# Gate/up and down as two passes over 512 tokens, weights loaded anew, seven PSUM banks in a ring, residual in bf16

## The chip, the core and the metric

The kernel runs on one core of a Trainium2 chip. A core has a matrix engine (PE in the profile, with its weight loads as PEld), a vector engine (DVE), a scalar engine (ACT), a general engine (POOL) and a queue engine that starts transfers (SP). Each executes its own instructions in the order in which the program wrote them; they wait for each other through semaphores. Data lie in SBUF, matrix products are summed in PSUM (eight banks of 512 fp32 numbers in each of 128 partitions). The metric is the device time of one execution in microseconds (us); before the change its median over 3 runs is 1082.35 us (1081.86 to 1082.96).

## What is computed

2048 tokens of width 576 pass through four layers: attention, gated unit, attention, gated unit, each with a layer norm in front and a residual sum behind. Both attention layers share their weights, and so do both gated units.

```python
x = x + A(layernorm(x))   # qkv = x @ wqkv (576 x 1728); 32 heads of 18; every token attends to
                          # 8 tokens: itself and those 2, 4, ... 14 before it; softmax; @ wo
x = x + B(layernorm(x))   # g = x @ w_gate; u = x @ w_up (576 x 4608); (g * u) @ w_down (4608 x 576)
```

The gated unit has most of the arithmetic; there is no nonlinear function in it, only the product `g * u`.

## The kernel before, in words

**Steps.** The tokens are cut into 18 steps: the first four of 128 tokens, the others of 256. The first half of the tokens passes both layers (steps 0 to 5 are attention layer 0 with its gated unit, 6 to 9 layer 1), then the second half (10 to 13, 14 to 17). `attention(j, ...)` and `glu(j, ...)` write the two halves of step `j`. All weights stay in SBUF, except `w_down`, which is loaded anew in each step, 18 tiles of 256 rows, into six buffers.

**Gate and up.** The 4608 inner columns are 36 column tiles of 128, and the 576 inputs are four full slices of 128 rows and one tail of 64. A unit is 512 PSUM columns of gate (one bank) and 512 of up (one bank): two column tiles at 256 tokens, four at 128. `full` (L788 to L796) multiplies the four full slices. `tails` (L798 to L809) multiplies the tails of two units at once: gate's 64 rows lie in the upper half of the array and up's in the lower, so that the two run side by side, in another division of the array than `full`. Units go in pairs: first one's `full`, `tails` of both, second one's `full`. In `evac` (L811 to L818) ACT copies g from PSUM to SBUF (L815) and DVE multiplies it with u out of PSUM (L816), which gives `h` in bf16.

**Down.** `down` (L826 to L836) multiplies `h` with `w_down` into `acc` (512 columns for each 128 tokens) and `acct` (the remaining 64). It runs behind the next pair's gate/up, in the same pass: pair by pair, gate/up and the down of the pair before alternate on PE. Gate/up has four PSUM banks, down three, and one, `pa`, is left to the small products of attention.

**Attention.** In `head` the layer norm (L353) is followed by a transpose, on PE in the first steps and by a DMA (L379) later. `project` (L458) computes q, k and v, in the same unit banks as gate/up. DVE forms q times k for the eight offsets (L580 to L590) in `prod` and `s1`; from step 5 on the sums over a head go through DRAM (`s_dram`, L641 to L647), softmax follows (L650 to L670), the weights go through DRAM once more (`a_dram` to `ab`, L691 to L694), DVE multiplies them with v and sums (L714, L731), PE multiplies with `wo` (L746), DVE adds the residual (L752), and the second `head` makes `xnT_B`, the input of the step's gated unit. The buffers `prod` and `s1` serve q times k, the returned parts, the softmax sums and the products with v of one step after the other; `a_c`, the weights, is a part of `s1`.

**Order.** `Plan` (L21 to L136) lists all operations with estimated costs, dependencies, priorities and buffers, and puts them in an order: each time it takes the operation that can start earliest. `bb` (L781) chains gate/up and down on PE in the order written; attention's products are put between them where their inputs and banks are planned to be ready, with margins (`mg`, 1500 ns in later steps). On the chip this order is fixed on each engine. Waits of SP for a buffer stand in the same queue as the transfers of attention.

Of the kernel before, what the change touches and what calls it, by code (L numbers as in the profile page):

```python
# [139 lines left out]
def kernel(  # L140
# [33 lines left out]
    NXS, NWD, NH, NXB = 4, 6, 4, 3  # L174
# [20 lines left out]
    wg = sb("wg", [P, KF, F])  # L195
    wu = sb("wu", [P, KF, F])
    wgu_t = sb("wgu_t", [P, F])
    Esel = sb("Esel", [P, 32])
    Bsel = sb("Bsel", [P, 4, 4, 32])
    xf = [sb(f"xf{i}", [P, NST, D], FP32) for i in range(NXS)]  # L200
    xb = [sb(f"xb{i}", [P, NST, D]) for i in range(2)]
    ob = [sb(f"ob{i}", [P, NST, D]) for i in range(2)]
# [7 lines left out]
    xnT_A = sb("xnT_A", [P, KT, CH])  # L210
    xnT_B = [sb(f"xnT_B{i}", [P, KT, CH]) for i in range(NXB)]
# [9 lines left out]
    wd = [sb(f"wd{i}", [P, 2, D]) for i in range(NWD)]  # L221

    pg = [psum.tile([P, 2 * CH], FP32, name=f"pg{i}") for i in range(2)]
    pu = [psum.tile([P, 2 * CH], FP32, name=f"pu{i}") for i in range(2)]
    acc = [psum.tile([P, 512], FP32, name=f"acc{i}") for i in range(NST)]
    acct = psum.tile([P, 512], FP32, name="acct")
    pa = psum.tile([P, 512], FP32, name="pa")

# [8 lines left out]
    banks = {"pa": [pa[:]], "boot": [acc[0][:], acc[1][:], acct[:]]}  # L237
    pool = {"k": "boot"}
# [24 lines left out]
    def load_x(t0, nst):  # L263
        b, i0 = (t0 // 2) % 2, t0 % 2
        if t0 == 2:
            op("POOL", 80, lambda: nc.gpsimd.memset(xb[b][0:1, i0, 0:2], 0.0), r=["wq3_0"], w=[f"xb{b}_{i0}"])
        o = op("SP", 600, dma(xb[b][:, i0:i0 + nst, :], xv[:, t0:t0 + nst, :]), w=[f"xb{b}_{i}" for i in range(i0, i0 + nst)],
               nbytes=P * nst * D * 2, prio=1.5 if t0 > 1 else 0, land=3000 if t0 else 1500, after=marks.get("x") if t0 == 3 else None)
        if t0 in (2, 3):
            marks["x"] = o  # L270
# [13 lines left out]
    def setup_b():  # L284
# [38 lines left out]
        def swap():  # L323
# [5 lines left out]
            late["a_c"] = late["s1"][:, 0:2 * CH]  # L329
            late["ab"] = rot.tile([P, 4, 2 * CH], BF16, name="ab")  # L330
        op("POOL", 0, swap, r=[f"wq{t}_{k}" for t in range(4) for k in range(KT)],
           w=["prod0", "prod1", "s10", "s11", "s12", "s13", "Lt", "ab"])
# [10 lines left out]
    def setup_glu():  # L343
        fw = F // FS
        for s in range(FS):
            fs = slice(s * fw, (s + 1) * fw)
            for nm, dst, src in (("wg", wg, B_w_gate), ("wu", wu, B_w_up)):
                op("SP", 500, dma(dst[:, :, fs], src[0:KF * P, fs].rearrange("(k p) f -> p k f", p=P)),
                   w=[f"{nm}{s}"], nbytes=P * KF * fw * 2, prio=4 + s, after=marks["x"])
            op("SP", 550, dma(wgu_t[0:TL, fs], B_w_gate[KF * P:D, fs]), w=[f"wgt{s}"], nbytes=TL * fw * 2, prio=4 + s, after=marks["x"])  # L350
            op("SP", 550, dma(wgu_t[TL:2 * TL, fs], B_w_up[KF * P:D, fs]), w=[f"wut{s}"], nbytes=TL * fw * 2, prio=4 + s, after=marks["x"])

    def head(src, keys, nst, dst, key, prio, ab, on_pe, mg, first=None, then=None):  # L353
# [18 lines left out]
        for i in range(nst):  # L372
# [5 lines left out]
            if not on_pe:  # L378
                op("SP", 900, lambda i=i: nc.sync.dma_start_transpose(out=dst[:, :, i * P:(i + 1) * P], in_=xn[i][:]),  # L379
                   r=[f"xn{ab}{i}"], w=[key + str(i)], prio=0, nbytes=P * KT * P * 2, land=2700)  # L380
                continue
# [6 lines left out]
            pl.also(o, [key + str(i)])  # L388
            o = op("ACT", 700, lambda i=i, b=b: nc.scalar.copy(dst[:, :, i * P:(i + 1) * P], bf(b())), r=[b.key], w=[key + str(i)],
# [49 lines left out]
    def attention(j, la, t0, nst):  # L439
        fast = j == 0  # L440
        z = j % 2
        qT, kT, vT = qT_[z], kT_[z], vT_[z]
# [4 lines left out]
        xs_b, xs_f = xb[(t0 // 2) % 2], xf[(t0 // 2) % NXS]  # L447
        bk = [f"xb{(t0 // 2) % 2}_{i0 + i}" for i in range(nst)]
        fk = [f"xf{(t0 // 2) % NXS}_{i0 + i}" for i in range(nst)]
        xin, xin_k = (xs_b, bk) if la == 0 else (xs_f, fk)  # L450
        xk = [f"xA{i}" for i in range(nst)]
        head(lambda i: xin[:, i0 + i, :], xin_k, nst, xnT_A, "xA", prio, 0, on_pe, mg, marks.get({2: "weights", 3: "sum"}.get(j)), marks["evac"] if j == 1 else None)
        op("ACT", 250, lambda: nc.scalar.copy(kT[:, :, 0:HALO], halo_k[la][:]), r=[f"halok{la}"], w=[f"kH{z}"], prio=prio)

        def bank(p_, u):
            return (pg, pu)[p_][u["slot"]]
# [69 lines left out]
        op("ACT", 250, lambda: nc.scalar.copy(vT[:, :, 0:HALO], halo_v[la][:]), r=[f"halov{la}"], w=[f"vH{z}"], prio=prio)  # L526
# [29 lines left out]
        else:  # L556
# [3 lines left out]
            project("a", uq, uv + ut, tq, ev_a, ev_b, [f"{x}{z}" for x in ("q0", "k0", "q2", "k2", "v0", "v2", "q4", "k4", "v4")])  # L560
        for d_, dst, hl in (("k", kT, halo_k), ("v", vT, halo_v)):
            op("ACT", 250, lambda hl=hl, dst=dst: nc.scalar.copy(hl[la][:], dst[:, :, n:n + HALO]),
               r=[f"{d_}{t}{z}" for t in range(0, KT, 2)], w=[f"halo{d_}{la}"], prio=prio)
# [7 lines left out]

        b1 = Bank()
# [357 lines left out]
```

## Time and profile before

| | |
|---|---|
| median of 3 runs | 1082.35 us |
| the profiled execution, its own time | 1079.86 us |
| span of its instructions | 1078.1 us |
| PE / DVE / ACT busy | 1063.8 / 755.1 / 369.4 us |
| matmuls | 10797 |
| `w_down` loads of 288 KB | 324 |
| first gate matmul / last matmul start | 32.7 / 1073.35 us |

The profile shows one execution. Its time is 1.8 us above its span (what lies around the first and the last instruction) and 2.5 us below the median of the runs. A row of a group names the source line, the engine, the operation, output and inputs with their shapes and the count; behind the bar come busy time in us and the mean of one in ns, then the idle time of the engine just before them with what ended it. A matmul's duration contains its way through the array, and matmuls overlap: what one costs in a sequence is read from one start to the next. A row of the timeline has start and duration in us; a row of the window table has the window, its length, and for each engine busy time and instructions. In the first 33 us the weights begin to arrive and the first attention runs; gate/up starts behind it.

### The profile page before, as it was taken

The numbers are of one execution on the slowest core, as the hardware profiler recorded it, in microseconds if no ns is written. First come the engines' busy times: TensorE is split into PE (matmuls) and PEld (weight loads), VectorE is DVE, ScalarE is ACT, GpSimd is POOL, SyncE is SP. The second block draws the span as 40 slices with busy tenths as digits, with TensorE's granted clock in tenths as the row PEclk, the third lists the DMA queues.
The fourth block names the chain that finished last, engine by engine and source line by source line (L and its number), as shares of the span: only waits on it lengthen the run. The fifth ranks groups of instructions, "written<-read, shape, count | busy, mean of one in ns | idle before, by whom it ended". The sixth has DMA issues, their size and how long they took to land.

```text
span 1078.1 us, 25413 instructions
## 1 busy us (share of the span) xinstructions
PE 1063.8 (99%) x10797; PEld 787.7 (73%) x10797; DVE 755.1 (70%) x1345; ACT 369.4 (34%) x756; POOL 8.8 (1%) x39
## 2 busy tenths in 40 slices
PE   8999999999999999999999999999999999999998
PEld 6788877777777777777777777777777777777775
DVE  7677987786959776685967778595876869472222
ACT  6544254332421544131242332423243332212121
POOL 3000000000000000000000000000000000000000
PEclk9999999999999999999999999999999999999999
DMA  9973774645263644435363734536353543534331
GB/s 278 342 208 92 208 175 122 169 105 138 79 169 105 153 115 108 126 112 150 109 170 97 162 93 121 134 84 170 89 153 91 127 116 106 157 112 112 101 110 56
DMA packets 155089, 146.16 MB, mean 136 GB/s; under 512 B 43104, under 2 KB 152672, under 8 KB 154976
## 3 DMA queue, kind: packets, MB, share of 16 engines
q1 hardware_dynamic: 154976, 144.55, 49.6%
q8 instruction: 84, 1.38, 0.5%
q14 instruction: 29, 0.24, 0.1%
HBM read 125.11 MB, written 10.88 MB: 126 GB/s over the span
## 4 chain that ended last, share of the span: by engine, by line
PE 95%; DMA 2%; DVE 2%; SPq 1%; issue 1%; ACT 0%; DVEq 0%; ACTq 0%
PE pg L793 24%; PE pu L793 23%; PE acc L832 23%; PE pg L804 7%; PE pg L469 5%; PE pu L469 4%; PE pa L746 4%; PE acct L834 3%; DMA wraw<-in_A_wqkv_dram 1%; DMA a_dram<-s 1%; DMA ab<-a_dram 1%; DVE h L816 0%; SPq L257 0%; DVE prod L714 0%; PE pa L680 0%
## 5 line engine op out<-in xcount | busy, mean ns | idle before, releaser
L816 DVE TENSOR_TENSOR h<-pu,g_sb 128x512 bf16<-128x512 f32 x288 | 196.3, 686 | 200.8 <-ACT g_sb L815 149.6
L815 ACT CAST g_sb<-pg 128x512 bf16<-128x512 f32 x288 | 168.2, 585 | 476.6 <-PE pu L804 391.3
L832 PE MATMUL acc<-wd,h 128*128 128x512 bf16 x1152 | 306.3, 380 | 0.0
L793 PE MATMUL pg<-xnT_B,wg 128*128 128x256 bf16 (+1 forms) x2592 | 300.8, 261 | 0.8 <-ACT xnT_B L431 0.8
L793 PE MATMUL pu<-xnT_B,wu 128*128 128x256 bf16 (+1 forms) x2592 | 299.3, 261 | 0.0
L793 PEld LDWEIGHTS <-wg 128*128 128x128 bf16 x2592 | 212.5, 98 | 61.2 <-issue 26.2
L793 PEld LDWEIGHTS <-wu 128*128 128x128 bf16 x2592 | 230.9, 98 | 23.3
L834 PE MATMUL acct<-wd,h 128*128 128x64 bf16 x1152 | 222.0, 193 | 0.0
L832 PEld LDWEIGHTS <-h 128*128 128x128 bf16 x1152 | 112.7, 98 | 117.9
L714 DVE TENSOR_TENSOR prod<-vT,ab 128x1280 bf16<-128x1280 bf16 (+1 forms) x127 | 92.9, 741 | 66.5 <-DMA ab<-a_dram 66.4
L469 PEld LDWEIGHTS <-wqkv 128*128 128x128 bf16 (+1 forms) x1260 | 95.4, 97 | 30.3 <-issue 16.1
L834 PEld LDWEIGHTS <-h 128*128 128x128 bf16 x1152 | 112.9, 98 | 2.2
L580 DVE TENSOR_TENSOR prod<-qT,kT 128x2560 bf16<-128x2560 bf16 (+1 forms) x72 | 95.5, 1331 | 1.0 <-ACT kT L522 0.4
L731 DVE TENSOR_TENSOR oT<-oT,prod 128x1280 bf16<-128x1280 bf16 (+1 forms) x119 | 90.8, 763 | 3.0
L804 PE MATMUL pu<-xnT_B,wgu_t 64*128 64x256 bf16 (+1 forms) x648 | 88.1, 260 | 0.0
L804 PE MATMUL pg<-xnT_B,wgu_t 64*128 64x256 bf16 (+1 forms) x648 | 88.0, 260 | 0.0
L469 PE MATMUL pg<-xnT_A,wqkv 128*128 128x256 bf16 (+3 forms) x650 | 79.7, 260 | 1.5 <-issue 0.9
L469 PE MATMUL pu<-xnT_A,wqkv 128*128 128x256 bf16 (+3 forms) x610 | 76.5, 262 | 2.6 <-DVE h L816 2.1
L804 PEld LDWEIGHTS <-wgu_t 64*128 64x128 bf16 x1296 | 47.0, 94 | 32.5 <-issue 27.8
L746 PE MATMUL pa<-wo_p,oT 128*128 128x288 bf16 x310 | 48.2, 286 | 0.1
L375 ACT ACTIVATE xn<-xf,nmr,rstd 128x576 bf16<-128x576 f32 x47 | 40.7, 866 | 8.8 <-DVE nmr L367 8.8
L584 DVE TENSOR_TENSOR prod<-prod 128x1024 bf16<-128x1024 bf16 (+1 forms) x64 | 41.1, 643 | 0.8
(117 smaller groups left out, 563.1 us busy)
## 6 DMA issues: line engine op xcount, KB each, us to landing
wd<-in_B_w_down_dram SPq DMA_DIRECT2D x324, 288.0 KB, 3.3
s_dram<-s SPq DMA_DIRECT2D x13, 512.0 KB, 3.7
prod<-s_dram SPq DMA_DIRECT2D x52, 128.0 KB, 2.9
ab<-a_dram SPq DMA_DIRECT2D x52, 128.0 KB, 2.7
wg<-in_B_w_gate_dram SPq DMA_DIRECT2D x6, 768.0 KB, 9.8
wu<-in_B_w_up_dram SPq DMA_DIRECT2D x6, 768.0 KB, 10.4
out_dram<-ob SPq DMA_DIRECT2D x8, 288.0 KB, 2.6
wraw<-in_A_wqkv_dram SPq DMA_DIRECT2D x4, 432.0 KB, 5.0
```

The lines of the kernel that those rows point to most:

```text
L469: nc.tensor.matmul(bank(p_, u)[0:m, e * n:(e + 1) * n], lhsT=wqkv[r_, k, c0:c0 + m], rhs=xnT_A[r_, k, 0:n], start=start, stop=stop, skip_g ...
L580: nc.vector.tensor_tensor(late["prod"][p_ % 2][:, :, :, 0:n], q2, k2, op=ALU.mult)
L584: nc.vector.tensor_tensor(prod[:, :, 0:4:2, 0:n], prod[:, :, 0:4:2, 0:n], prod[:, :, 1:4:2, 0:n], op=ALU.add)
L714: nc.vector.tensor_tensor(js(dst), js(vT[:, :, o0:o0 + n]), abw, op=ALU.mult)
L731: op("DVE", 60 + 3 * n, lambda i_=i_: nc.vector.tensor_tensor(oT[:, :, 0:n], oT[:, :, 0:n], late["prod"][i_ % 2][:, 0, :, 0:n], op=ALU.add ...
L746: nc.tensor.matmul(b()[:, 0:HD], lhsT=oT[:, t, i * P:(i + 1) * P], rhs=wo_p[:, t, hh * HD:(hh + 1) * HD], start=(t == 0), stop=(t == KT - 1))
L793: nc.tensor.matmul(pt[:, e * n:(e + 1) * n], lhsT=w_[:, k, ft * P:(ft + 1) * P], rhs=xT[:, k, 0:n], start=(first and k == 0 and e == 0), s ...
L804: nc.tensor.matmul(ps[:, e * n:(e + 1) * n], lhsT=wgu_t[r_, ft * P:(ft + 1) * P], rhs=xT[r_, KF, 0:n], start=(first and e == 0), stop=not ...
L815: op("ACT", 590, lambda: nc.scalar.copy(g_sb[gs][:, 0:ul], pg[use["slot"]][:, 0:ul]), r=[f"wg_{j}_{u}"], w=[f"g{gs}"], prio=0)
L816: op("DVE", 690, lambda: nc.vector.tensor_tensor(hb[hs][:, 0:ul], pu[use["slot"]][:, 0:ul], g_sb[gs][:, 0:ul], op=ALU.mult), r=[f"wu_{j}_{ ...
L832: nc.tensor.matmul(acc[i][:], lhsT=lhs, rhs=wt[:, e % 2, 0:512], start=(ft == 0), stop=(ft == NFT - 1))
L834: nc.tensor.matmul(acct[:, i * TL:(i + 1) * TL], lhsT=lhs, rhs=wt[:, e % 2, 512:D], start=(ft == 0 and i == 0), stop=(ft == NFT - 1), skip ...
```

## The change

Steps 0 to 5 stay in form. Everything after them (12 steps of 256 tokens) becomes six blocks of 512 tokens, `big`, in the order layer/chunk (1,0), (0,2), (0,3), (1,1), (1,2), (1,3).

- A block has two passes. In the first, each of the 36 column tiles is multiplied with all 512 tokens (one bank for gate, one for up, matmuls of 512 columns), and the product is kept in SBUF for all tiles. In the second, down runs over the product in groups of four column tiles, for each of four 128-token tiles, into five banks.
- The product lies in the lower half of `reg`, where three of the six weight slices lie in the steps before. Each block starts with the three slices in the upper half; when one has been used, one of the other three is loaded into its place. Two more `w_down` buffers lie in what the product leaves free.
- PSUM: seven banks are one ring (`ring`), for gate/up, q/k/v and down alike. `pa` stays.
- `batch` puts three units together with one change to the tails. The q/k/v products of the next block's two steps are units of this block (four for each step, alternating with gate/up units from the first tile on); before, they were placed by the plan.
- Evacuation: ACT copies u as well and DVE multiplies in SBUF in all units of steps 0 to 5 and in two of three units of the blocks (`evacuate`).
- `prod`, `s1`, `a_c` and the returned parts (`rg`) get their own places; the layer norm's output `xnT_A` gets two buffers. The parts are added in three operations of 512 in place of one of 1024 and one of 512.
- x is loaded into `xf` itself, one tile pair for all 2048 tokens, in bf16, which serves as residual and as output; `xb`, `ob` and the fp32 `xf` go.

```diff
-    NXS, NWD, NH, NXB = 4, 6, 4, 3
+    NWD, NH = 6, 4
+    SC = 512
...
+    BLK, JOB_AT = 4, (0, 2)
...
-    xf = [sb(f"xf{i}", [P, NST, D], FP32) for i in range(NXS)]
+    xf = [sb(f"xf{i}", [P, NST, D]) for i in range(NTT // NST)]
...
+    ring = [pg[0], pu[0], pg[1], pu[1], pg[2], pu[2], acct]
...
+            late["a_c"] = rot.tile([P, 2 * CH], BF16, name="a_c")
+            late["rg"] = rot.tile([P, 8 * CH], BF16, name="rg")
...
+        def lp(p_):
+            return p_ % 2 if pe_sum else 0
...
-            pvk = f"pv{i_ % 4}" if fast else f"prod{i_ % 2}"
+            pvk = f"pv{i_ % 4}" if fast else f"pq{i_ % 2}"
+
+            def tmp(i_=i_, half=half):
+                return late["prod"][i_ % 2][:, half, :, 0:n] if fast else late["prod"][1][:, i_ % 2, :, 0:n]
...
+    def evacuate(bk, keys, dst, dk, ul, act, fg, fu):
+        gs = unit_no["n"] % 2
+        unit_no["n"] += 1
+        op("ACT", 590, lambda: nc.scalar.copy(g_sb[gs][:, 0:ul], bk(0)[:, 0:ul]), r=[keys[0]], w=[f"g{gs}"], prio=0, **fg)
+        if act:
+            op("ACT", 590, lambda: nc.scalar.copy(dst, bk(1)[:, 0:ul]), r=[keys[1]], w=[dk], prio=0, **fu)
+            op("DVE", 340, lambda: nc.vector.tensor_tensor(dst, dst, g_sb[gs][:, 0:ul], op=ALU.mult), r=[f"g{gs}"], w=[dk], prio=0)
+        else:
+            op("DVE", 690, lambda: nc.vector.tensor_tensor(dst, bk(1)[:, 0:ul], g_sb[gs][:, 0:ul], op=ALU.mult),
+               r=[keys[1], f"g{gs}"], w=[dk], prio=0, **fu)
...
+    def batch(us):
+        closing, opening = us[:2], us[2:]
+        for u in closing:
+            u["full"](True, False)
+
+        def fn():
+            for u in us:
+                u["tails"](u in opening)
+        for u in opening:
+            for x in u["use"]:
+                take(x)
...
+        for u in closing:
+            u["evac"]()
+        for u in opening:
+            u["full"](False, True)
+            u["evac"]()
...
+    def big(sc, la, t0, jobs):
...
+        res = sorted((i for i in loc if loc[i] >= FS // 2 and owner.get(loc[i], i) == i), key=lambda i: loc[i])
+        oth = [i for i in range(FS) if i not in res]
+        order = [ft for i in res + oth for ft in range(i * FSL, (i + 1) * FSL)]
...
+                            nc.tensor.matmul(ring[use[q]["slot"]][:], lhsT=w_[:, k], rhs=xT[:, k], start=(first and k == 0),
+                                             stop=(last_ and k == KF - 1), skip_group_check=True)
...
+                evacuate(lambda p_: ring[use[p_]["slot"]], keys, hv(ft), f"hh{ft}", SC, m % 3 > 0, fg, fu)
...
+        starts = dict(zip(JOB_AT, jobs))
+        ready = []
+        for m, ft in enumerate(order):
+            if m in starts:
+                units = []
+                gen = prepare(starts[m], units)
+                next(gen)
+                units[-1]["done"].append(lambda gen=gen: next(gen, None))
+                ready += units
+            if ready:
+                push(ready.pop(0))
+            u = g_unit(m, ft)
+            i = ft // FSL
+            if i in res and ft % FSL == FSL - 1:
+                new = oth[res.index(i)]
+
+                def swap_in(i=i, new=new):
+                    slot = loc[i]
+                    owner[slot] = new
+                    load_weights(new, slot, 4, marks["x"])
+                u["done"].append(swap_in)
+            push(u)
...
+        nb = NFT // BLK
+        for b in range(nb):
+            for i in range(NSC):
+                def fn(b=b, i=i):
+                    for q in range(BLK):
+                        ft = order[b * BLK + q]
+                        wt, lhs = wdb[bufs[ft // 2]], hv(ft)[:, i * P:(i + 1) * P]
...
+                        nc.tensor.matmul(bank_of(i)[:], lhsT=lhs, rhs=wt[:, ft % 2, 0:512], start=first, stop=last_)
+                        nc.tensor.matmul(bank_of(NSC)[:, i * TL:(i + 1) * TL], lhsT=lhs, rhs=wt[:, ft % 2, 512:D],
+                                         start=(first and i == 0), stop=last_, skip_group_check=True)
...
+    for j in range(JSM, JSM + 2):
+        for _ in prepare(j):
+            pass
     while pend:
         pend.pop(0)()
...
+    for sc in range(2, len(order_sc)):
+        j = JSM + 2 * (sc - 2)
+        big(sc, seq[j][0], seq[j][1], [q for q in (j + 2, j + 3) if q < len(seq)])
```

More of the change, by code (lines that the diff above doesn't have):

```diff
@@ L446, in attention @@
         i0 = t0 % 2
[L447 to L453, printed above, removed]
@@ L884 @@
+    pend = []
+    nsc = NTT // NSC
+    order_sc = [(0, 0), (0, 1), (1, 0), (0, 2), (0, 3), (1, 1), (1, 2), (1, 3)]
+    assert nsc == 4 and n_al == 2
+    seq = [(0, t, 1) for t in range(NSC)]
+    for l, c in order_sc[1:]:
+        seq += [(l, c * NSC + t, NST) for t in range(0, NSC, NST)]
+    JSM = 6
     marks = {}
```

381 lines of the change are left out of this document (263 added, 118 removed).

## The prediction

> **What bounds the kernel now.** I read the page first: who is busy, at which clock, and what the chain that ended last consists of.
>
> ```profile
> span 1078.1 us, 25413 instructions
> PE 1063.8 (99%) x10797; PEld 787.7 (73%) x10797; DVE 755.1 (70%) x1345; ACT 369.4 (34%) x756; POOL 8.8 (1%) x39
> PEclk9999999999999999999999999999999999999999
> PE 95%; DMA 2%; DVE 2%; SPq 1%; issue 1%; ACT 0%; DVEq 0%; ACTq 0%
> ```
>
> PE is busy almost from end to end at full clock, and 95% of the chain is PE. So time can be saved only where PE needs less of it for the same columns, and lost wherever PE has to wait. How tightly PE runs is seen in its timeline; this is one cycle (a pair of units, then the down of the pair before):
>
> ```profile
> 486.32 1.04 PE L793 MATMUL pg<-xnT_B,wg 128*128 128x256 bf16 x8
> 487.19 1.04 PE L793 MATMUL pu<-xnT_B,wu 128*128 128x256 bf16 x8
> 488.16 0.28 PE L804 MATMUL pg<-xnT_B,wgu_t 64*128 64x256 bf16 x1
> ...
> 488.71 1.05 PE L793 MATMUL pg<-xnT_B,wg 128*128 128x256 bf16 x8
> 489.59 1.04 PE L793 MATMUL pu<-xnT_B,wu 128*128 128x256 bf16 x8
> 490.46 0.38 PE L832 MATMUL acc<-wd,h 128*128 128x512 bf16 x1
> 490.68 0.19 PE L834 MATMUL acct<-wd,h 128*128 128x64 bf16 x1
> 490.71 0.38 PE L832 MATMUL acc<-wd,h 128*128 128x512 bf16 x1
> ...
> 492.42 1.04 PE L793 MATMUL pg<-xnT_B,wg 128*128 128x256 bf16 x8
> ```
>
> The starts are what counts: eight full matmuls of 256 columns take 0.87 us (0.109 each); the eight down pairs from 490.46 to 492.42 take 0.245 each, of which the 64-column one has 0.029, so one of 512 columns has 0.216. The four tail pairs take 0.55 where four times 0.109 is 0.44, and the eight full ones before them 0.97 where 0.87 is usual: one trip to the tails and back costs 0.10 + 0.11 = 0.21 us beyond its columns. There is no other hole in the cycle. Last, the second half in windows of one step each, and the attention chain on DVE in one of them:
>
> ```profile
> 402.00:464.00 62.00, 61.89 (x569) 45.55 (x568) 43.42 (x73) 19.96 (x40) 0.00 (x0) 1.00 0.46 117
> ...
> 896.00:959.00 63.00, 63.00 (x577) 45.17 (x575) 44.26 (x75) 14.83 (x27) 0.00 (x0) 1.00 0.46 131
> sum 557.00, PE 555.21 PEld 403.33 DVE 408.89 ACT 178.18 POOL 0.00; mean PE 61.69 PEld 44.81 DVE 45.43 ACT 19.80 POOL 0.00
> ```
>
> ```profile
> 463.65 1.48 DVE L580 TENSOR_TENSOR prod<-qT,kT 128x2560 bf16<-128x2560 bf16 x1
> ...
> 482.63 0.42 DVE L590 TENSOR_TENSOR s<-s,prod 128x512 bf16<-128x512 bf16 x1
> ...
> 491.36 1.23 DVE L650 TENSOR_TENSOR prod<-prod 128x1024 f32<-128x1024 bf16 x1
> ...
> 499.06 0.69 DVE L670 TENSOR_TENSOR s<-Lt,zs 128x512 bf16<-128x512 f32 x1
> ...
> 508.44 1.56 DVE L714 TENSOR_TENSOR prod<-vT,ab 128x1280 bf16<-128x1280 bf16 x2 [4.80 <-DMA ab<-a_dram]
> ...
> 524.20 0.83 DVE L731 TENSOR_TENSOR oT<-oT,prod 128x1280 bf16<-128x1280 bf16 x1
> 524.94 1.48 DVE L580 TENSOR_TENSOR prod<-qT,kT 128x2560 bf16<-128x2560 bf16 x1
> ```
>
> A step takes 557/9 = 61.9 us, DVE is busy 45.4 of it. One step's attention holds DVE's buffers from 463.65 to 525.0, and the next step's begins that moment: attention is serial, 61 us a step, just PE's pace. Before, its result is needed only a step at a time.
>
> **The change on PE (what sets the end).** Per block of 512 tokens, against two steps:
> - Full slices: 2 x 36 x 8 = 576 matmuls x 0.109 = 62.8 us become 288 x 0.216 = 62.2: 0.6 saved.
> - Tails: 72 pairs x 0.109 = 7.9 become 36 x 0.216 = 7.8: 0.1 saved.
> - Trips: two steps have 2 x 9 for gate/up and 2 x 2 for q/k/v, 22. A block has 36 + 8 units in threes, 15; the last, without attention, 12 against 18. That is 7 x 0.21 = 1.5 us (1.3 in the last).
> - Down, q/k/v and `wo`: the same matmuls, in another order, 0.
> Five blocks x 2.2 and 2.1 for the last are 13.1 us. Two steps are 123.8 us now, so a block is 121.6.
>
> **What moves on the other engines.**
>
> ```profile
> L816 DVE TENSOR_TENSOR h<-pu,g_sb 128x512 bf16<-128x512 f32 x288 | 196.3, 686 | 200.8 <-ACT g_sb L815 149.6
> L815 ACT CAST g_sb<-pg 128x512 bf16<-128x512 f32 x288 | 168.2, 585 | 476.6 <-PE pu L804 391.3
> L584 DVE TENSOR_TENSOR prod<-prod 128x512 bf16<-128x512 bf16 x8 | 3.3, 416 | 0.1
> L375 ACT ACTIVATE xn<-xf,nmr,rstd 128x576 bf16<-128x576 f32 x47 | 40.7, 866 | 8.8 <-DVE nmr L367 8.8
> L376 ACT ACTIVATE xn<-xf,nmr,rstd 128x64 bf16<-128x64 f32 x47 | 20.1, 428 | 0.0
> wd<-in_B_w_down_dram SPq DMA_DIRECT2D x324, 288.0 KB, 3.3
> wu<-in_B_w_up_dram SPq DMA_DIRECT2D x6, 768.0 KB, 10.4
> ```
>
> The product from SBUF has the row of 512 bf16 numbers, 0.42 us, in place of 0.69. DVE per block: two attentions of 45.4 - 18 x 0.69 = 33.0, then 12 x 0.69 + 24 x 0.42 = 18.4, and four copies of q/k/v parts a step, some 8 x 0.59 = 4.7 by ACT's row: 89 of 121.6 us, against 91 of 123.8. ACT gets 24 x 0.59 = 14 us more and gives 4.7 away: 49 of 121.6. Both are covered by PE as long as their work comes in time; if DVE's cover is gone, see the rivals.
>
> Weights: the reload is three slices of 2 x 768 and 2 x 96 KB, 5.2 MB a block; `w_down` is loaded once, not twice, 5.2 MB less. A slice is requested after its predecessor's sixth column tile and used 12 tiles (over 23 us) later; a load of this size landed in 10.4 us. Cost 0; without that cover, up to 10 us a slice. On SP's queue its four issues stand ahead of attention's transfers (the bounces through DRAM, the transposes), and their bytes ahead of those: 0 to 4 us on attention, not on PE. `w_down` in the second pass: two loads (3.3 us) per four tiles (3.9 us), with eight buffers full at its start: 0.
>
> PSUM: seven banks for three units. After a trip the next unit needs one bank at once (the seventh, free) and its second 0.87 us later, when ACT has had time for one copy of 0.59. Best 0, worst an `xn` pair of 0.87 + 0.43 in front, less the slack, 0.4 us, eight times a block, 3.2. I take 0.2 a block, near the best: the row of L815 shows ACT idle 476.6 us before these copies. At the change of pass five banks are needed, three are free and one more is wanted per 0.98 us: 0.
>
> A rule that speaks against the change: the Trainium skill, "TensorE: Matmul & The Clock Gate", section "A second HAM failure mode: psum-queue depth-cycling", has a kernel with 512-column matmuls cycling through PSUM banks whose small idle moments made the clock fall to half and rise again. Here the 512-column matmuls of down already run at 0.216 us with the clock at 9 in all slices, so the trace does not bear it out; by the rule the time would be the last rival's.
>
> Hand-over from the steps to the blocks: the first block needs step 7's attention whole, a step earlier than now.
>
> ```profile
> 33.00:340.00 307.00, 306.15 (x3704) 235.42 (x3702) 237.33 (x442) 119.87 (x257) 0.00 (x0) 1.00 0.57 157
> 33.00:316.00 283.00, 48.70 (x72) 1.00 0.58 159
> 338.98 0.81 DVE L731 TENSOR_TENSOR oT<-oT,prod 128x1280 bf16<-128x1280 bf16 x1
> L379 SPq DMA_TRANSPOSE xnT_B<-xn x2: 1207/1888/2569, 357.5 to 360.4; - x2
> DMA to landing us min/median/max: 2.6/3.6/4.5
> 315.64 1.04 PE L793 MATMUL pg<-xnT_B,wg 128*128 128x256 bf16 x8
> ```
>
> The first row is all engines, the second DVE's products of steps 0 to 5 alone. Step 7's last sum ends at 339.8 and its transposes land at about 364 (360.4 + 3.6), 24 us later; PE begins step 6 at 315.64, and with the last down and `wo` of step 7 would arrive at about 320. DVE's work up to 339.8 is 237 - 49 + 72 x 0.42, less some 5 us of step 6's products: 213 us. Its own buffers let the next step's q times k start during the bounces, so DVE need not stay 77% busy: at 77% step 7 is done at 33 + 277 + 24 = 334 (PE waits 14), at 90% at 33 + 237 + 24 = 294 (no wait). I take 2 us, nearer the second, since the serial chain was what left DVE idle.
>
> The end: behind the last matmul DVE has 0.69 + 2 x 0.28 instead of 2 x 0.69 + 0.28, 0.4 us less, and one more transfer to issue: 0.
>
> **Sum.** 13.1 - 2 - 6 x 0.2 = 10 us. The profiled execution would be 1079.86 - 10 = 1070; the median stands 2.5 above it, so 1082.35 - 10 = 1072.
>
> **Rivals.**
> 1. Attention late at each block, slower. Both of the next block's attentions start inside this block and must end in it. A step's chain from 463.65 to its landed transposes (below) is 543.4 + 3.5 - 463.7 = 83 us.
>
> ```profile
> L379 SPq DMA_TRANSPOSE xnT_B<-xn x2: 1222/1416/1610, 539.9 to 543.4; - x2
> DMA to landing us min/median/max: 3.2/3.5/4.3
> ```
>
> Its q/k/v units end about 12 us (first) and 31 us (second: 16 units of 1.95) into the block. Best: 31 + 83 = 114, 7 us early. Worst, serial as now: 12 + 61 + 83 = 156, 34 late, five times. Against it: q times k, returned parts, weights and v products no longer share buffers, and 89 us of DVE fit into 121.6. For it: reloads in front of the bounces, and DVE has no other attention to do when the second bounces. Half-way late, 8 us x 5, gives 1069 + 40 = 1109; it decides from 13/5 = 2.6 us late per block.
> 2. The hand-over waits for its full 14 us: 1069 + 14 + 1 = 1084; against it the arithmetic above.
> 3. Banks are not free in time: 3.2 us a block, 19, gives 1069 + 19 + 2 = 1090. For it: before, down stood between gate/up units and gave the copies 2 us; in the first pass nothing does.
> 4. PE falls to a slow clock after waits. The start shows it:
>
> ```profile
> 1.37 4.88 PE L759 MATMUL pa<-ident 128*128 128x128 bf16 x44 [1.37 <-POOL ident L275]
> 6.57 0.90 PE L759 MATMUL pa<-ident 128*128 128x128 bf16 x13
> ```
>
> 44 matmuls at 0.108 us, later ones at 0.054: 2.4 us lost per such stretch. Once at each of twelve passes: 29 us, 1072 + 29 = 1101.
>
> **How the numbers follow.** Forecast 0.57 (its own range 1066 to 1079); rival 1 0.16; rival 2 0.14, in part only; rival 3 0.08; rival 4 0.05. About 0.2% (2 us) is what a measurement can tell from no change. Faster: the forecast, and half of rivals 2 and 3 where the wait stays under 11 us: 0.57 + 0.08 = 0.65. The same, 1080 to 1084.5: 0.07, from rivals 2 and 3. Slower: 0.28, rivals 1 and 4 and the rest. The predicted time is the forecast's, 1072. Low is no wait at all and another 4 us from what I set at nothing, 1065; high takes in rivals 2 and 3 and the beginning of 1, 1092, and leaves out its later part and rival 4.
>
> **What would show it.** Right: 512-column gate/up matmuls 0.216 us apart, 87 trips from the third step of 256 tokens on, blocks of about 122 us, PE without idle time between blocks, 216 `w_down` loads. Wrong: PE waiting for `xnT_B` or at the first gate of a block (rival 1), a hole of over 5 us near 320 us (2), PE waiting for ACT's copies in the first pass (3), 512-column matmuls 0.43 apart (4). The forecast fails if these waits add up to more than 11 us.

## The result and the profile after

The changed kernel takes 1066.51 us, the median of 4 runs (1065.30 to 1069.22). The kernel before took 1082.56 us beside it (1081.86 to 1082.96). The ratio is 0.9856 with a 95% interval of 0.9836 to 0.9876, so the change saves 16 us. The forecast was 1072, with a range of 1065 to 1092. The profiled execution of the changed kernel took 1067.05 us, its span 1065.3 us: 12.8 us less than the profiled span before.

The page of the changed kernel, first the busy times, then the granted clock in 40 slices, then the shares of the chain:

```profile
span 1065.3 us, 20911 instructions
PE 1041.1 (98%) x8503; PEld 604.2 (57%) x8637; DVE 726.5 (68%) x1398; ACT 449.1 (42%) x932; POOL 8.9 (1%) x39
PEclk9999999999999999999999999999999999999999
PE 90%; DVE 4%; DMA 3%; issue 1%; ACT 1%; SPq 1%; DVEq 0%; ACTq 0%
L866 DVE TENSOR_TENSOR reg<-reg,g_sb 128x512 bf16<-128x512 bf16 x144 | 60.0, 420 | 27.4 <-ACT reg L865 27.4
wd<-in_B_w_down_dram SPq DMA_DIRECT2D x188, 288.0 KB, 3.3
reg<-in_B_w_down_dram SPq DMA_DIRECT2D x28, 288.0 KB, 3.1
```

PE is still the engine that sets the time, at full clock. It has 2160 weight loads fewer. DVE's product from SBUF takes 0.420 us, where the product from PSUM took 0.686. The `w_down` loads are 188 + 28 = 216.

The timeline of PE in the first pass of a block (start, duration, line, tiles, count):

```profile
455.20 0.60 PE L484 MATMUL pg<-xnT_A,wqkv 128*128 128x256 bf16 x4
455.64 0.60 PE L484 MATMUL pu<-xnT_A,wqkv 128*128 128x256 bf16 x4
456.08 0.60 PE L484 MATMUL pg<-xnT_A,wqkv 128*128 128x256 bf16 x4
456.51 0.60 PE L484 MATMUL pu<-xnT_A,wqkv 128*128 128x256 bf16 x4
456.95 1.03 PE L1015 MATMUL pu<-xnT_B,reg 128*128 128x512 bf16 x4
457.81 1.03 PE L1015 MATMUL pg<-xnT_B,reg 128*128 128x512 bf16 x4
```

Read the starts: four matmuls of 512 columns take 457.81 - 456.95 = 0.86 us, 0.215 each, and four of 256 columns take 0.44. There is no hole between the units.

The blocks, cut where one block's second pass ends; columns are us, busy time and count for PE, PEld, DVE, ACT and POOL, granted clock, DMA share, GB/s:

```profile
443.77:570.83 127.06, 126.01 (x814) 63.64 (x829) 89.16 (x159) 46.37 (x96) 0.00 (x0) 1.00 0.45 126
570.83:698.01 127.18, 126.13 (x814) 63.64 (x829) 92.71 (x173) 49.64 (x104) 0.00 (x0) 1.00 0.43 122
...
952.12:1060.20 108.08, 107.30 (x639) 48.05 (x650) 21.80 (x43) 31.66 (x60) 0.00 (x0) 1.00 0.28 88
```

A block takes 127 us and PE works through it; the 1 us that is not busy fits records that are missing (814 matmuls beside 829 weight loads; where none are missing, as with six banks below, PE is busy for the whole block). DVE has 89 to 93 us of work in it, ACT 46 to 50. The last block has no attention and takes 108.

The hand-over from the steps to the blocks, PE's timeline again:

```profile
315.88 0.60 PE L484 MATMUL pg<-xnT_A,wqkv 128*128 128x256 bf16 x4
...
317.19 0.60 PE L484 MATMUL pu<-xnT_A,wqkv 128*128 128x256 bf16 x4
318.73 1.02 PE L1015 MATMUL pg<-xnT_B,reg 128*128 128x512 bf16 x4 [0.95 <-DMA xnT_B<-xn]
```

PE waits 0.95 us for step 7's transposes. Between blocks the wait does not appear. These are the transposes that the block from 570.83 on needs:

```profile
L395 SPq DMA_TRANSPOSE xnT_B<-xn x2: 1199/1224/1248, 556.2 to 557.5; - x2
DMA to landing us min/median/max: 2.9/3.3/3.6
```

With 1.2 us for the issue and at most 3.6 to landing, the second is there by about 557.5 + 1.2 + 3.6 = 562, and the next block's first gate starts at 572.8: attention is some 10 us early.

The twelve runs of the unaltered changed kernel lie between 1065.2 and 1069.6 us, seven of them below 1067.1 and five above 1068.6. In its three profiles the time from the end of the first block to the last matmul is the same, 616.0 to 616.1 us; the first block ends at 442.2, 444.0 or 446.6 us, so the differences arise before that. The last section shows one source of them.

### The profile page after: what moved, and what is told of

Same layout as the page of the kernel before. It is cut to its first block, busy times and chain, and to the rows that moved or that the text cites. A ratio compares the mean times of both kernels' runs of the same rounds, so it can differ in the third digit from the quotient of the medians.

```text
span 1065.3 us, 20911 instructions
## 1 busy us (share of the span) xinstructions
PE 1041.1 (98%) x8503; PEld 604.2 (57%) x8637; DVE 726.5 (68%) x1398; ACT 449.1 (42%) x932; POOL 8.9 (1%) x39
## 4 chain that ended last, share of the span: by engine, by line
PE 90%; DVE 4%; DMA 3%; issue 1%; ACT 1%; SPq 1%; DVEq 0%; ACTq 0%
PE pg L1015 15%; PE pu L1015 15%; PE pg L1088 8%; PE pu L1088 6%; PE acct L1015 5%; PE pg L892 5%; PE pu L892 5%; PE acct L1088 4%; PE pa L817 3%; PE pg L928 3%; PE pg L484 3%; PE pu L484 3%; PE pg L1024 2%; PE pu L1024 2%; PE pu L1089 2%; PE pg L531 2%
## 5 line engine op out<-in xcount | busy, mean ns | idle before, releaser
L1015 PEld LDWEIGHTS <-reg 128*128 128x128 bf16 x1728 | 163.3, 98 | 207.4 <-issue 26.0
L1015 PE MATMUL pg<-xnT_B,reg 128*128 128x512 bf16 x727 | 184.7, 380 | 2.6 <-DMA xnT_B<-xn 0.9
L1015 PE MATMUL pu<-xnT_B,reg 128*128 128x512 bf16 x712 | 183.0, 380 | 1.8 <-issue 1.0
L863 ACT CAST g_sb<-pg 128x512 bf16<-128x512 f32 x166 | 97.9, 592 | 153.5 <-PE pu L904 73.4
L1088 PEld LDWEIGHTS <-reg 128*128 128x128 bf16 x864 | 84.4, 98 | 101.9 <-issue 2.1
L892 PEld LDWEIGHTS <-reg 128*128 128x128 bf16 x1728 | 119.2, 98 | 16.3 <-issue 4.5
L786 DVE TENSOR_TENSOR prod<-vT,ab 128x1280 bf16<-128x1280 bf16 (+1 forms) x127 | 93.2, 740 | 13.3 <-DMA ab<-a_dram 13.2
L1089 PEld LDWEIGHTS <-reg 128*128 128x128 bf16 x864 | 84.8, 98 | 0.6
L1089 PE MATMUL pu<-wd,reg 128*128 128x64 bf16 x416 | 80.2, 193 | 0.8
L892 PE MATMUL pg<-xnT_B,reg 128*128 128x128 bf16 (+1 forms) x864 | 75.7, 238 | 0.8 <-ACT xnT_B L447 0.8
L1088 PE MATMUL pg<-wd,reg 128*128 128x512 bf16 x280 | 75.9, 380 | 0.0
L892 PE MATMUL pu<-xnT_B,reg 128*128 128x128 bf16 (+1 forms) x864 | 75.4, 237 | 0.0
L928 PE MATMUL pg<-wd,h 128*128 128x512 bf16 x192 | 63.6, 380 | 0.1
L1015 PE MATMUL acct<-xnT_B,reg 128*128 128x512 bf16 x232 | 62.3, 380 | 0.7
```

The source lines that it names most:

```text
L786: nc.vector.tensor_tensor(js(dst), js(vT[:, :, o0:o0 + n]), abw, op=ALU.mult)
L863: op("ACT", 590, lambda: nc.scalar.copy(g_sb[gs][:, 0:ul], bk(0)[:, 0:ul]), r=[keys[0]], w=[f"g{gs}"], prio=0, **fg)
L892: nc.tensor.matmul(pt[:, e * n:(e + 1) * n], lhsT=w_[:, k], rhs=xT[:, k, 0:n], start=(first and k == 0 and e == 0), stop=(last_ and k == K ...
L928: nc.tensor.matmul(acc[i][:], lhsT=lhs, rhs=wt[:, e % 2, 0:512], start=(ft == 0), stop=(ft == NFT - 1))
L1015: nc.tensor.matmul(ring[use[q]["slot"]][:], lhsT=w_[:, k], rhs=xT[:, k], start=(first and k == 0), stop=(last_ and k == KF - 1), skip_grou ...
L1088: nc.tensor.matmul(bank_of(i)[:], lhsT=lhs, rhs=wt[:, ft % 2, 0:512], start=first, stop=last_)
```

## The experiments

Where an experiment's difference is small, it is taken against 1066.6 us, the median of the 12 timed runs of the unaltered changed kernel, and against the block period, which is the same to 0.1 us in its three profiles. A median can stand up to 3 us off because of the spread just told: beside the set in which the unaltered kernel had 1069.08, the batches of two and the matmuls of 256 columns would be 5.8 and 1.8 us slower, not 8.3 and 4.3. The block period carries the argument there.

**The changed kernel again, unaltered.**

> The changed kernel unaltered, to see the size of the change beside fresh runs of the kernel before. By the sum of the prediction (trips to the tails 8.6 us, full matmuls of 512 columns 3.6, tails 0.8, no waits) it is 13 us faster than before, ratio 0.988; by the first four runs it is 16 us faster, ratio 0.9856. If the sum is complete, the profiled span is 12 to 14 us under that of before and what is left of the 16 lies in the clock or around the span, not in PE's sequence; if something is missing from the sum, PE's sequence from 316 us on is 16 us shorter than before.

Measured: 1069.08 us (1065.52 to 1069.59), ratio 0.9867 [0.9849, 0.9885]. A third set gave 1065.78 (1065.16 to 1069.04), 0.9857 [0.9840, 0.9874]. The gain is there each time; 3 us of it depend on the run.

> The changed kernel unaltered once more, on the same chip, as the measure for the kernel without the two waits: 1065 to 1070, with runs near 1065.5 where the wait near 180 us is short and runs near 1069 where the clock falls behind it.

**Trips to the tails: batches of two units, not three.**

```diff
-            if len(bat) == 3:
+            if len(bat) == 2:
```

> Units in the blocks go in twos in place of threes: 22 trips to the tails per block in place of 15 (last block 18 for 12), 41 more in all; matmuls, columns and everything else stay. Theory (a trip costs 0.21 us): 8.6 us slower than the changed kernel, about 1075. Rival (the gain is in the wide matmuls and the trips cost nothing, or are hidden): no change, 1066 to 1068. If the missing third unit also makes PE wait for banks, more than 9 us, and PE shows holes behind the tails.

Measured: 1074.88 us (1074.06 to 1079.02), ratio 0.9934 [0.9916, 0.9951], 8.3 us above 1066.6. Two of its blocks:

```profile
445.98:574.51 128.53, 127.69 (x814) 62.47 (x828) 89.45 (x159) 46.18 (x96) 0.00 (x0) 1.00 0.44 125
574.51:703.04 128.53, 127.69 (x814) 62.48 (x828) 93.02 (x173) 49.35 (x104) 0.00 (x0) 1.00 0.43 120
```

The same matmuls take 128.53 us instead of 127.06: 1.47 us for 7 more trips, 0.21 each. That is the price read from the starts in the profile before. Over six blocks it makes 8.6 us (1.27 in the last). PE also waits 1.0 us at a `wo` in the first block; between the two profiled spans the difference is 9.2 us.

**Matmuls of 256 columns in the blocks.**

```diff
-  nc.tensor.matmul(ring[use[q]["slot"]][:], lhsT=w_[:, k], rhs=xT[:, k], ...)
+  for c in (0, 256):
+      nc.tensor.matmul(ring[use[q]["slot"]][:, c:c + 256], lhsT=w_[:, k], rhs=xT[:, k, c:c + 256], ...)
```

> In the first pass each matmul of 512 columns is cut into two of 256 with the same weights, tails too; 1728 full ones become 3456, as before the change. Theory (0.109 for 256 against 0.216 for 512): 4.2 us slower than the changed kernel, about 1070 to 1071. Rival (the wide matmuls are the main gain, because a weight load of 98 ns hardly fits behind a matmul of 256 columns): 10 us or more. No difference at all (under 2 us) would say that the size of the matmul does not matter.

Measured: 1070.85 us (1069.71 to 1073.06), ratio 0.9893 [0.9876, 0.9910], 4.3 above 1066.6. One of its blocks:

```profile
445.90:573.76 127.86, 127.49 (x1183) 95.32 (x1189) 89.24 (x159) 46.50 (x96) 0.00 (x0) 1.00 0.45 126
```

It takes 127.86 us, where it was 127.06. So the width of the matmuls is worth 0.8 us a block; it is not what made the most of the gain.

**The two passes' attention made serial.** The change gave the products of q and k a buffer of their own; here the sum over v's products also waits for that buffer, as it did before.

```diff
-  ALU.add), r=[pvk], w=["oT"], prio=prio)
+  ALU.add), r=[pvk, "prod0"], w=["oT"], prio=prio)
```

> The sums of the products with v are made readers of the buffer of q times k, so that the next step's q times k begins only when the last sum of the step before is done, as in the kernel before; the memory itself stays divided, DVE's work is the same. Theory (the divided buffers are what lets two attentions fit into a block): second attention of a block starts q times k some 55 to 61 us behind the first, ends 75 to 83 us later, 15 to 28 us behind the end of the 127 us block, in five blocks: 75 to 135 us, and the hand-over waits some 15 us; 1150 to 1215 in all. Rival (DVE with 73% has room, order does not matter): under 5 us, about 1070.

Measured: 1186.49 us, ratio 1.0959 [1.0936, 1.0981], clock 0.945. From the timeline of DVE in one block, the first attention's last sum and the second's first product, which now come one after the other:

```profile
561.96 0.82 DVE L802 TENSOR_TENSOR oT<-oT,prod 128x1280 bf16<-128x1280 bf16 x1
562.71 1.48 DVE L649 TENSOR_TENSOR prod<-qT,kT 128x2560 bf16<-128x2560 bf16 x1
```

In a block of the changed kernel the second attention's first product starts before the first attention's first sum, 48 us before its last one:

```profile
471.24 1.49 DVE L649 TENSOR_TENSOR prod<-qT,kT 128x2560 bf16<-128x2560 bf16 x1
499.31 0.83 DVE L802 TENSOR_TENSOR oT<-oT,prod 128x1280 bf16<-128x1280 bf16 x1
519.40 0.83 DVE L802 TENSOR_TENSOR oT<-oT,prod 128x1280 bf16<-128x1280 bf16 x1
```

With the serial order 18 to 20 us pass between the last down of each block and the first gate of the next, in which PE has only `wo` and a few q/k/v products, and the first gate of the blocks comes at 349.88 us, 31 us later than in the changed kernel. The clock is at half in about 130 us of the span, part of it while PE stands, so that the 120 us are waits and slow clock together. Without the overlap of the two attentions the change would be a loss of 10%.

**Attention begun later in the block**: after 8 and 10 column tiles instead of 0 and 2.

```diff
-    BLK, JOB_AT = 4, (0, 2)
+    BLK, JOB_AT = 4, (8, 10)
```

> The next block's two attentions start at the ninth and eleventh gate/up tile in place of the first and third, eight tiles or some 16 us later; all work stays. In the changed kernel the second attention's transposed input lands about 10 us before the next block's first gate needs it (issued 558.7, landing about 562, first gate 572.7). Theory (attention runs through at its own pace): it comes 6 to 8 us late in five blocks, 30 to 40 us in all, 1097 to 1107. Rival (the plan or a quieter DVE catches up): under 10 us.

Measured: 1113.11 us (1112.07 to 1114.14), ratio 1.0279 [1.0246, 1.0313]. The timeline of PE at one change of block, and the transposes it waits for:

```profile
581.86 0.19 PE L1089 MATMUL pu<-wd,reg 128*128 128x64 bf16 x1
587.22 2.29 PE L1015 MATMUL pu<-xnT_B,reg 128*128 128x512 bf16 x5 [5.17 <-DMA xnT_B<-xn]
```

```profile
L395 SPq DMA_TRANSPOSE xnT_B<-xn x2: 1206/1216/1227, 583.1 to 584.4; - x2
```

The five waits are 7.2, 5.4, 5.3, 7.0 and 7.0 us from the start of the last down to the first gate. That is the slack of 10 us used up and exceeded, as expected. After the wait shown five matmuls take 2.29 us, nearly twice what they take at full clock. Of the 46.5 us over 1066.6 the five waits make 31.8. The hand-over waits 2.70 us, where it was 0.95. The granted clock was at half for 37.5 us in all, which costs up to 18.8 and covers what is left, some 13. The mechanism was expected; that the clock drops behind it was not, and puts the time above the expected range.

**The product straight from PSUM on DVE**, without ACT's copy of u.

```diff
-        if act:
+        if False:
```

> ACT no longer copies u; DVE multiplies out of PSUM in all units, as before the change. DVE gets 24 x 0.27 = 6.5 us more per block and 72 x 0.27 = 19 us more in steps 0 to 5. Theory (DVE sets the pace of attention, PE only waits where attention is late): blocks keep their 127 us because 10 us were to spare; the hand-over, where nothing is to spare, waits 10 to 20 us more: 1075 to 1087. Rival 3 of the prediction in another form (banks come free too late): PE waits in the first pass of each block, block length over 128.5 us.

Measured: 1097.54 us (1096.58 to 1098.64), ratio 1.0136 [1.0114, 1.0157]. That is above the expected range. The blocks keep their 127.06 us; nearly all that is lost is lost at the hand-over, as the windows show:

```profile
320.00:330.00 10.00, 0.00 (x0) 0.00 (x0) 9.79 (x15) 0.00 (x0) 0.00 (x0) 0.58 0.25 84
330.00:340.00 10.00, 5.45 (x20) 2.68 (x20) 8.37 (x24) 3.29 (x8) 0.00 (x0) 0.50 0.00 0
340.00:350.00 10.00, 3.25 (x8) 1.05 (x8) 3.73 (x14) 2.78 (x6) 0.00 (x0) 0.50 0.17 33
350.00:360.00 10.00, 10.00 (x69) 5.86 (x69) 5.05 (x7) 3.97 (x9) 0.00 (x0) 0.88 0.01 2
```

PE stands and DVE works on step 7's attention; the first gate of the blocks comes at 346.75 instead of 318.73, 28 us later, where 10 to 20 were expected. The forecast had taken 0.27 us off each of 72 products of steps 0 to 5, 19 us of DVE, for this very place; the run shows that the hand-over wait would have been large without it. The upper bound of 14 us that I gave that wait holds only with the shorter products.

**Six banks instead of seven.**

```diff
-    ring = [pg[0], pu[0], pg[1], pu[1], pg[2], pu[2], acct]
+    ring = [pg[0], pu[0], pg[1], pu[1], pg[2], pu[2]]
```

> The ring has six banks in place of seven (acct's is left idle in the blocks). Theory (copies are done 0.8 us after a trip and the next bank is needed 1.7 us after it): 0 to 4 us slower, 1067 to 1072. Rival (the ring is tight, the seventh bank is what keeps PE going): PE waits for one more copy at each of 87 trips, 0.5 us or more each, over 40 us.

Measured: 1069.00 us (1066.20 to 1069.54), ratio 0.9867 [0.9843, 0.9890]; the blocks behind the first take 127.06 us as with seven. A window over one of them:

```profile
443.00:571.00 128.00, 128.00 (x839) 64.20 (x838) 89.29 (x159) 46.43 (x96) 0.00 (x0) 1.00 0.44 126
```

In the first block PE waits for banks in one place. Its timeline there, and what ACT does at that time:

```profile
375.33 0.37 PE L1024 MATMUL pu<-xnT_B,reg 64*128 64x512 bf16 x1 [0.30 <-DVE reg L868]
378.19 1.67 PE L1015 MATMUL pg<-xnT_B,reg 128*128 128x512 bf16 x7 [0.65 <-ACT g_sb L863]
```

```profile
375.38 0.87 ACT L391 ACTIVATE xn<-xf,nmr,rstd 128x576 bf16<-128x576 bf16 x1 [1.10 <-DVE nmr L383]
376.15 0.42 ACT L392 ACTIVATE xn<-xf,nmr,rstd 128x64 bf16<-128x64 bf16 x1
376.48 0.85 ACT L391 ACTIVATE xn<-xf,nmr,rstd 128x576 bf16<-128x576 bf16 x1
```

This is the worst case that the prediction named, an `xn` pair in front of a copy; here it is two pairs. From its first gate to its last down this block takes 126.9 us, where it takes 125.3 in all three profiles of the changed kernel. So the seventh bank is worth 1.6 us, once, which the medians can't tell from the spread; everywhere else six are enough.

**No reload of weights.** The loads of the last three slices are left out, so that the first three slices' weights stand in their place.

```diff
-                    load_weights(new, slot, 4, marks["x"])
+                    loc[new] = slot
```

> No weight slice is loaded anew: the last three slices of a block are multiplied with the weights that lie in the upper half already (so these products, and the output, are not the reference's; amounts of work stay). 5.2 MB a block less to move. Theory (the loads are hidden, PE sets the time): within 2 us of the changed kernel, 1065 to 1069; attention's transposes issue up to 4 us earlier in the block. Rival (the loads cost time): 5 us or more faster.

Measured: 1066.40 us (1065.19 to 1070.47), ratio 0.9858 [0.9825, 0.9890]; the blocks again 127.06 us. The transposes for the second block are issued at 553.4 and 555.3 instead of 556.2 and 557.5:

```profile
L395 SPq DMA_TRANSPOSE xnT_B<-xn x2: 1199/1200/1202, 553.4 to 555.3; - x2
```

The block itself begins 0.85 us earlier in this run (the last down before it starts at 443.16, not 444.01). So the reload delays attention by 1.4 to 2.0 us, inside its 10 us of slack, and costs nothing.

**The kernel before, with ACT's copy of u alone.** Here the kernel before gets one part of the change: u is copied from PSUM by ACT, and DVE multiplies in SBUF.

```diff
-  op("DVE", 690, lambda: nc.vector.tensor_tensor(hb[hs][:, 0:ul], pu[...], g_sb[gs][:, 0:ul], op=ALU.mult), ..., free="unit", use=use)
+  op("ACT", 590, lambda: nc.scalar.copy(hb[hs][:, 0:ul], pu[...]), ..., free="unit", use=use)
+  op("DVE", 340, lambda: nc.vector.tensor_tensor(hb[hs][:, 0:ul], hb[hs][:, 0:ul], g_sb[gs][:, 0:ul], op=ALU.mult), ...)
```

> The kernel before with one part of the change alone: ACT copies u out of PSUM too and DVE multiplies in SBUF; no blocks, no ring, no wide matmuls. PE's sequence before has four waits of 0.8 us in the tails of q/k/v where the unit bank is held until DVE has multiplied (0.80 us where 0.006 is usual, near 389, 572, 697 and 821 us). Theory (the part of the gain that the sum did not contain is these waits, and they go because ACT frees the banks): the waits are gone, 3 to 4 us faster than before, 1078 to 1079. Rival (they go only because q/k/v stand in the chain of the block): the waits stay, within 2 us of before. In a third case ACT's second copy or a new order makes it slower.

Measured: 1076.74 us (1075.85 to 1078.50) beside 1080.31, ratio 0.9963 [0.9949, 0.9976]: 3.6 us saved. The kernel before has waits of PE inside its q/k/v tails, first in the timeline, then as its group on the page (busy, mean ns, idle before and what ended it):

```profile
572.28 0.28 PE L469 MATMUL pg<-xnT_A,wqkv 64*128 64x256 bf16 x1
573.08 0.27 PE L469 MATMUL pu<-xnT_A,wqkv 64*128 64x256 bf16 x1 [0.52 <-DVE h L816]
```

```profile
L469 PE MATMUL pu<-xnT_A,wqkv 128*128 128x256 bf16 (+3 forms) x610 | 76.5, 262 | 2.6 <-DVE h L816 2.1
```

And the same group with ACT's copy:

```profile
L469 PE MATMUL pu<-xnT_A,wqkv 128*128 128x256 bf16 (+3 forms) x610 | 76.3, 262 | 0.4 <-ACT wqkv L307 0.3
```

A unit of q/k/v waited there for a bank that DVE had still to multiply out of. There are four such gaps of 0.80 us between starts (near 389, 572, 697 and 821 us). The next pair usually starts 0.11 us behind, so each costs 0.69; with one of 0.27 near 696 they make 3.0 of the 3.6 us, and all have gone. ACT's copy is enough to end them, but it is not the only way: in the run with the product straight from PSUM the blocks have no such gap either, with seven banks and q/k/v in one sequence with gate/up.

**A version without the two holes.** The step whose layer norm PE waits for near 178 us gets a longer lead in the order, and the first block begins with two q/k/v units, so that PE has work while step 7's transposes land.

```diff
-  head(lambda i: xs_f[:, i0 + i, :], fk, nst, xT, xTk, prio - 1, 1, on_pe, mg)
+  head(lambda i: xs_f[:, i0 + i, :], fk, nst, xT, xTk, prio - 1, 1, on_pe, 2800 if j == 4 else mg)
...
-            if ready:
-                push(ready.pop(0))
+            for _ in range(2 if sc == 2 and m == 0 else 1):
+                if ready:
+                    push(ready.pop(0))
```

> Two waits of PE are filled: the transposes of step 4's second layer norm get a margin of 2.8 us in place of 0.5 (in the changed kernel PE waits 1.1 to 2.1 us for them near 178 us), and the first block begins with two q/k/v units in place of one (PE waits 1.2 us for step 7's input near 318 us). The work stays. Theory: 2 to 3 us less waiting, and no stretch at half clock near 180 us, which follows where that wait is 2.1 us long: 1063.5 to 1066, and the spread between runs gets smaller, against a median of 1067.8 of the changed kernel's eight runs so far. Rival (the waits only move on, to step 4's input or the hand-over): no difference, 1066 to 1069.

> The kernel with the two waits filled once more. If filling them takes the slower runs away, no run above 1067 again, where five of twelve runs of the changed kernel were above 1068.5; if the first four runs were luck, one or two of these lie near 1069.

Measured: 1065.73 us (1065.10 to 1066.25), ratio 0.9852 [0.9835, 0.9868], and again 1063.04 (1062.54 to 1064.99) beside 1080.31, ratio 0.9841 [0.9826, 0.9855]. Both holes are gone from the traces; the first run's profile has a wait of 1.2 us for a `wo` near 189 us instead, the second's has not. None of its nine runs was in the group near 1069, against five of twelve of the changed kernel. In the one set that both shared, the medians are 1065.73 and 1065.78, and the intervals overlap: that it is steadier is shown by few runs, that its median is lower is not settled.

## Why the prediction was right, point by point

- **What it starts from.** Right. PE bounds both kernels, and the gain is time that PE had spent beside its columns. From 315.6 us to the start of the last matmul PE needed 1073.35 - 315.6 = 757.7 us before and 1060.11 - 315.6 = 744.5 after. By the weight loads recorded behind 315.6 us, the new kernel then still had 56 full and 7 pairs of tail q/k/v matmuls more to do, and 20 `wo` and 7 pairs of down fewer: 6.1 + 0.8 - 2.4 - 1.7 = 2.8 us more. So 13.2 + 2.8 = 16 us were saved in this part.
- **Trips, tails and full slices, 13.1 us.** Right. There are 87 trips in the trace after, as forecast. The price of a trip is borne out by the batches of two (1.47 us for 7), the width by the matmuls of 256 columns (0.8 us a block, where 0.6 and 0.1 were forecast).
- **A term was missing: 3.6 us.** "There is no other hole in the cycle" was read from a cycle without q/k/v. The row of the q/k/v group with 2.1 us ended by the product of DVE stood on the page, and that the new copies would free those banks sooner was not priced: the part on ACT and DVE called both "covered by PE". The run with ACT's copy alone measures it. The range took it in because its lower end allowed 4 us for what was set at nothing; the forecast itself did not.
- **Hand-over, 2 us of 0 to 14.** It measured 0.95. The sign and the size were right, but the figures behind it were partly lucky: I let PE arrive "at about 320", and it arrives about 317.7. Step 7's attention was in at 318.7, inside the two estimates of 294 and 334. The run with the product from PSUM shows how steep this is: 28 us for 0.27 us on each product.
- **PSUM, 0.2 us a block.** It is 0 with seven banks. With six, the worst case came once, in the first block, and cost 1.6 us.
- **Reload of weights, 0, and 0 to 4 us on attention.** Right: 0, and 1.4 to 2.0 us on attention.
- **"Two steps are 123.8 us now, so a block is 121.6".** Wrong, a block is 127.06. I divided the 557 us from 402 to 959 by nine, the number of attentions in them (180 `wo` matmuls, 20 a step). By their weight loads these windows hold 2496 full gate/up matmuls, 8.67 steps of 288, and 430 full q/k/v ones, 7.7 steps of 56. What is missing to nine steps is 0.33 x 9 cycles x 6.10 us (the cycle of the timeline before, 486.32 to 492.42) = 18 us, and 1.3 x 7.3 = 9.5 us of q/k/v (56 and 14 matmuls at 0.109, less half of the 14 that run as pairs, and two trips). Two steps are thus (557 + 28)/9 x 2 = 130.0 us, and less the 2.2 and the q/k/v waits in these windows (0.6 in two steps), 127.2: the block, within 0.2. The saving was worked out by counts and is untouched. The error made rival 1 look nearer than it was: the real block gives attention 5 us more.
- **Attention in time (the forecast against rival 1).** Right. The transposes land 562 - 443.8 = 118 us into the block; my best case was 114, and the worst, serial, 156. The serial run and the late start show that this is where the change would have failed, and at what point: an attention about 10 us later.
- **The end.** Set at 0; it is 0.4 us longer. Behind the last matmul's start come 1065.3 - 1060.11 = 5.2 us, where it was 1078.1 - 1073.35 = 4.8.
- **Sum.** 13.1 + 3.6 - 0.95 = 15.8 us against the 16 read above. The start up to 315.6 us is 2.8 us behind in columns, which the forecast did not have, and the end 0.4: 15.8 - 2.8 - 0.4 = 12.6, against 12.8 between the two profiled spans. The median moved by 16, because the medians stand differently to the profiled executions. So the forecast of 10 was too small by the missing term and by the two waits that came out shorter (1.05 at the hand-over, 1.2 at the banks).
- **The chances.** Half of rivals 2 and 3 is (0.14 + 0.08)/2 = 0.11; the sum for "faster" used 0.08. No reading changes by it.

Rivals 2 and 3 did not come about. The waits of rival 4 did not come either, since the blocks have no wait after which the clock falls; outside them the one near 178 us does it in some runs (last section). The rule that I had set beside it, the Trainium skill, "TensorE: Matmul & The Clock Gate", section "A second HAM failure mode: psum-queue depth-cycling", is not borne out by the blocks: they cycle 512-column matmuls through seven banks at a granted clock of 1.00.

## What to carry to other kernels

On a kernel that PE bounds at full clock, look for what PE spends beside columns: count the changes between full and 64-row matmuls and price one by the starts, and look in each kind of unit, not only in the commonest, for banks that are freed late. When work is gathered into larger blocks, the deadline of everything that feeds a block moves together; work out when the last input lands from the chain, and remove what made that chain serial (here one shared buffer, worth 120 us) in the same change. Take the pace of a stage from its own counts, not from a window divided by the number of another engine's rounds.

## What the runs showed of the hardware

A short wait of PE costs more than itself from some length on. Near 178 us PE waits for a layer norm. PE's timeline there, of the changed kernel's profile:

```profile
178.31 0.22 PE L904 MATMUL pu<-xnT_B,reg 64*128 64x128 bf16 x1
179.39 0.56 PE L402 MATMUL pa<-ident,xn 128*128 128x128 bf16 x5 [0.86 <-ACT xn L391]
```

and of the unaltered kernel's second profile, in the same place:

```profile
177.80 0.22 PE L904 MATMUL pu<-xnT_B,reg 64*128 64x128 bf16 x1
179.87 0.62 PE L402 MATMUL pa<-ident,xn 128*128 128x128 bf16 x5 [1.86 <-ACT xn L391]
```

The windows of that second profile behind it (granted clock is the third column from the end):

```profile
178.00:182.00 4.00, 1.92 (x14) 1.12 (x14) 3.94 (x7) 3.40 (x8) 0.00 (x0) 0.77 0.32 105
182.00:186.00 4.00, 4.00 (x36) 2.93 (x35) 3.92 (x6) 2.28 (x5) 0.00 (x0) 0.80 0.27 78
```

After 0.86 us of waiting the clock stays at 1.00; after 1.86 us 3.4 us pass at half clock, up to 1.7 us lost on top of 1.0 us more wait. Other runs have waits in between and above, here the longest with a named cause that left the clock at 1.00 (the version without the two holes) and two that did not (the product straight from PSUM, the late start):

```profile
189.20 0.79 PE L817 MATMUL pa<-wo_p,oT 128*128 128x288 bf16 x5 [1.16 <-DVE oT L802]
184.26 1.14 PE L892 MATMUL pg<-xnT_B,reg 128*128 128x256 bf16 x8 [2.00 <-ACT xnT_B L405]
316.47 1.02 PE L1015 MATMUL pg<-xnT_B,reg 128*128 128x512 bf16 x4 [2.70 <-DMA xnT_B<-xn]
```

The last two were each followed by 3.4 us at half clock, which began 0.8 and 1.0 us after PE had started again (0.3 us after the wait of 1.86). Where between 1.16 and 1.86 us it begins, and whether the length of the wait alone decides, is not shown.

This is one of the sources of the spread of 4 us between runs, and the granted clocks of the twelve runs fit it: 0.996 to 0.998 in the five above 1068.6 us, 0.999 to 1.000 in the other seven. I have seen the wait in these two profiles, and do not know what makes ACT's layer norm later in some runs. It is not the only source: the profiles with six banks and with 256 columns have 6.8 us at half clock before the first 26 us are over. The waits of 5.3 to 7.2 us at the block changes of the late start brought 3.4 to 10.2 us at half clock, and the late hand-over with the product from PSUM 30.7 us, part of it while PE stood. Every stretch at half clock behind the first 30 us lasts 3.41 us or a whole multiple of it, within 0.05 us: 3.4, 6.8 and 10.2 with the late start, 30.7 = 9 x 3.41 here, 17.1 and 20.5 in the serial run. The Trainium skill, "TensorE: Matmul & The Clock Gate", section "What's actually happening", says that the clock goes back to half after an idle window of about 3.4 us, in windows that run freely; the stretches of 3.41 us and its multiples agree with its window, but the drop here came after a wait of 1.9 us, well under one.
